# Roots by GpSimd pow, a halved first unit and lighter clock-warming matmuls in a fused spectral filter and gated MLP kernel

## The chip, the cores and the metric

The kernel runs on one core of one Trainium2 chip. The metric is device time in microseconds (us) of one execution. The span of a profile is about 1.7 us shorter than the time of the same execution (before: 177.5 against 179.18). All runs used here are fast runs; the single slow one (a run of the kernel before at 262.98 us, granted clock 0.661) is left out.

## The reference, cut to what matters

```python
xn = layernorm(x)                                   # x: 2048 rows x 512, bf16
A  = irfft2(rfft2(xn) * (w_r + 1j * w_i))           # spectral filter
h  = gelu(xn @ w_gate) * (xn @ w_up)                # 512 -> 1792
out = x + A + h @ w_down                            # 1792 -> 512
```

The kernel does the transforms as matmuls too. The 2048 rows are 16 chunks of 128. Each chunk needs mean and variance (DVE), a reciprocal root `rstd`, the normalised rows `xn`, and their transpose `xnT`. Chunks 0 to 3 are normalised on DVE and transposed on TensorE (PE). Chunks 4 to 15 come in three groups of four: the root and the bias `nb = -mean*rstd` on GpSimd (POOL), `xn` on ACT, the transpose by DMA.

Of the kernel before, what the change touches and what calls it, by code (L numbers as in the profile page):

```python
# [10 lines left out]
P = 128  # L11
# [6 lines left out]
S = 2048  # L18
D = 512
# [182 lines left out]
def kernel(  # L202
# [53 lines left out]
    def load_w(a, b, eng=nc.sync):  # L256
        nc.sync.dma_start(out=Wg_sb[:, :, a:b], in_=wg_v[:, :, a:b])
        eng.dma_start(out=Wu_sb[:, :, a:b], in_=wu_v[:, :, a:b])
# [3 lines left out]
    root = pc.tile([P, 1], F32, name="root")  # L262
    nc.vector.memset(spin[:], 0.0)
    nc.vector.memset(eps_t[:], EPS)
    ident_t = pc.tile([P, P], BF16, name="ident_t")
# [7 lines left out]
    def load_w(T, a, b, eng=nc.sync):  # L273
        v = wg_v if T is Wg_sb else wu_v
        return eng.dma_start(out=T[:, :, a:b], in_=v[:, :, a:b])

    pin = tc.keep_in_program_order
    pin(nc.scalar.activation(out=root[:], in_=eps_t[:], func=AF.Sqrt, bias=eps_t[:], scale=1.0))
    load_x(0, 1)
    load_x(1, 1)  # L280
# [19 lines left out]
    LAND = {0: 2.9, 1: 3.5, 2: 8.8, 3: 8.8}  # L300
    LAND.update({c: 12.6 if c < 8 else 18.5 if c < 12 else 21.5 for c in range(4, NC)})
    WG_LAND = [6.6] * 4 + [10.2] * 4 + [15.0] * 6
    WU_LAND = [8.0] * 4 + [11.7] * 4 + [17.0] * 6
    RF_LAND = 20.0

# [5 lines left out]

    ident = ident_t[:]
# [4 lines left out]
    for k in range(25):  # L317
        pin(nc.tensor.matmul(sp_ps[:, :P if k < 20 else D], lhsT=spin[:], rhs=spin[:] if k < 20 else x_t[:, 0, :],
                             start=True, stop=True))

    def spin_on():
        for k in range(6):
            nc.tensor.matmul(sp_ps[:, :256], lhsT=spin[:], rhs=x_t[:, 0, :256], start=True, stop=True)
# [31 lines left out]
    def rsqrt_steps(U, c0, n):  # L355
        y = rstd[:, c0:c0 + n]
        v = pc.tile([P, n], F32, name=f"v{c0}")
        t = pc.tile([P, n], F32, name=f"t{c0}")

        def first():  # L360
            U.tensor_scalar(out=v[:], in0=mv[:, c0:c0 + n, 1], scalar1=EPS, scalar2=None, op0=ALU.add)
            U.tensor_scalar(out=y.bitcast(I32), in0=v[:].bitcast(I32), scalar1=-0.5, scalar2=float(0x5F1FFFF9),
                            op0=ALU.mult, op1=ALU.add)

        def newton(a, k):
            U.tensor_tensor(out=t[:], in0=y, in1=y, op=ALU.mult)  # L366
            if U is V:
                U.scalar_tensor_tensor(out=t[:], in0=v[:], scalar=-a, in1=t[:], op0=ALU.mult, op1=ALU.mult)
                U.scalar_tensor_tensor(out=y, in0=t[:], scalar=k, in1=y, op0=ALU.add, op1=ALU.mult)
                return  # L370
            U.tensor_tensor(out=t[:], in0=v[:], in1=t[:], op=ALU.mult)
            U.tensor_scalar(out=t[:], in0=t[:], scalar1=-a, scalar2=k, op0=ALU.mult, op1=ALU.add)
            U.tensor_tensor(out=y, in0=t[:], in1=y, op=ALU.mult)

        def bias():
            b = nb[:, c0:c0 + n]
            U.tensor_tensor(out=b, in0=mv[:, c0:c0 + n, 0], in1=y, op=ALU.mult)
            U.tensor_scalar(out=b, in0=b, scalar1=-1.0, scalar2=None, op0=ALU.mult)  # L378

        steps = [first, lambda: newton(0.703952253, 0.703952253 * 2.38924456), lambda: newton(0.5, 1.5)]  # L380
        return steps + ([] if U is V else [bias])
# [3 lines left out]
    def first_two():  # L385
        o = {}

        def v(k, fn, occ, deps=(), lat=None, t_min=0.0):
            o[k] = add("DVE", occ, fn, [o[d] for d in deps], key=-2000 + len(o), lat=lat, t_min=t_min,
                       after=o.get("last"))  # L390
            o["last"] = o[k]

        def root_of(c):
            o["root", c] = add("ACT", 0.31, lambda: A.activation(
                out=rstd[:, c:c + 1], in_=mv[:, c, 1:2], func=AF.Sqrt, bias=eps_t[:], scale=1.0),
                [o["mean", c]], key=-2000 + c)

        def T(c, h):
            o["T", c, h] = add("PE", 0.12, lambda: f_T(c, 2 * h, 2), [o["xn", c, h]], key=-2000 + 2 * c + h,
                               lat=0.36, acq=("S",))  # L400

        def recip(c):
            v(("rstd", c), lambda: V.reciprocal(out=rstd[:, c:c + 1], in_=rstd[:, c:c + 1]), 0.15, [("root", c)])

        def xn_(c, h):
            v(("xn", c, h), lambda: f_norm_v(c, 256 * h, 256), 0.27, [("rstd", c)], lat=0.4)

        def copy(c, h):
            v(("copy", c, h), lambda: f_Tc(c, 2 * h, 2), 0.25, [("T", c, h)], lat=0.4)
            o["copy", c, h].rel = ("S",)  # L410

        def stats(c):
            v(("stats", c), lambda: f_stats(c), 0.6, t_min=LAND[c], lat=0.7)

        def mean(c):
            v(("mean", c), lambda: f_mean(c), 0.1, [("stats", c)])
            root_of(c)

        stats(0)
        mean(0)  # L420
        stats(1)
        recip(0)
        xn_(0, 0)
        mean(1)
        xn_(0, 1)
        table = add("ACT", 1.3, lambda: None, [o["root", 1]], key=-1500, lat=1.3)
        T(0, 0)
        T(0, 1)
        add("PE", 0.65, spin_on, [o["T", 0, 1]], key=-1500, lat=0.65, after=o["T", 0, 1])
        copy(0, 0)  # L430
        copy(0, 1)
        recip(1)
        v("xn1", lambda: f_norm_v(1, 0, D), 0.33, [("rstd", 1)], lat=0.45)
        t = add("PE", 0.23, lambda: f_T(1, 0, NE), [o["xn1"]], key=-1998, lat=0.45, acq=("S",))
        xT_op[0], xn_op[0] = o["copy", 0, 1], o["xn", 0, 1]
        xT_op[1] = add("ACT", 0.5, lambda: f_Tc(1, 0, NE, A.copy), [t, table], key=-1200, rel=("S",))
        xn_op[1] = o["xn1"]

    first_two()
# [5 lines left out]
    hold = {}  # L445

    def second_two():
        m = [moments(c, -1200 + c) for c in (2, 3)]
        steps = rsqrt_steps(V, 2, 2)
        m = [add("DVE", 1.5, lambda: [f() for f in steps], m, key=-1190)]  # L450
        hold[0] = m[0]
        for c in (2, 3):
            xn_op[c] = add("DVE", 0.33, lambda c=c: f_norm_v(c, 0, D), m, key=-1180 + c, lat=0.53)
            hold[1] = xn_op[c]
            t = add("PE", 0.23, lambda c=c: f_T(c, 0, NE), [xn_op[c]], key=-880 + c, lat=0.5, acq=("S",))
            e, f = ("ACT", A.copy) if c == 2 else ("DVE", V.tensor_copy)
            xT_op[c] = add(e, 0.5, lambda c=c, f=f: f_Tc(c, 0, NE, f), [t], key=-1100 + c, rel=("S",))
# [3 lines left out]
    def later_four(c0, km, kx):  # L461
        m = [moments(c, km + 0.1 * c) for c in range(c0, c0 + 4)]
        for k, f in enumerate(rsqrt_steps(nc.gpsimd, c0, 4)):
            m = [add("POOL", (0.8, 1.15, 1.15, 0.7)[k], f, m, key=c0 + k,
                     lat=(0.8, 1.15, 1.15, 0.9)[k])]
        for c in range(c0, c0 + 4):
            xn_op[c] = add("ACT", 0.72, lambda c=c: A.activation(  # L467
                out=xn[:, c, :], in_=x_t[:, c, :], func=AF.Identity, bias=nb[:, c:c + 1],
                scale=rstd[:, c:c + 1]), m, key=kx + 0.1 * c)
            xT_op[c] = add("SP", 1.3, lambda c=c: nc.sync.dma_start_transpose(  # L470
                out=xnT[c // 4][:, :, c % 4, :], in_=xn[:, c, :]), [xn_op[c]], key=c, lat=4.0, t_min=25.0)
# [13 lines left out]
    def unit(k, c0, n, f0, m=1):  # L485
# [21 lines left out]

        def f_ge():
            b["ge"] = pw.tile([P, m, w], BF16, name="ge", bufs=3)
            A.activation(out=b["ge"][:], in_=b["g_ps"][:], func=AF.Gelu_apprx_tanh)  # L510
# [8 lines left out]
        def split(name, tag, W_, key, t, h):  # L519
            o = None  # L520
            for f in range(0, m, h):
# [4 lines left out]
        g = split("g_ps", "G", Wg_sb, 1000 + k, WG_LAND, 2 if k == 0 else m)  # L526
        u = split("u_ps", "U", Wu_sb, 1000.5 + k, WU_LAND, 1 if k == 2 else m)
        ge = add("ACT", {1: 0.28, 2: 0.36, 4: 0.5}[n * m], f_ge, [g], key=-1000 + k,
                 lat={1: 0.38, 2: 0.48, 4: 0.7}[n * m], acq=("ge",), rel=("G",))
        h = add("DVE", {1: 0.21, 2: 0.34, 4: 0.61}[n * m], f_h, [ge, u], key=-1000 + k, rel=("U", "ge"),  # L530
                after=hold.get(k))
# [277 lines left out]
    def down(c):  # L809
# [7 lines left out]
        def mm(o, w):  # L817
            b[o] = ps.tile([P, w], F32, name="y_ps", tag="S", bufs=4)
            for f in range(NFC):
                T_.matmul(b[o][:], lhsT=hT_of(sb, f, 1, cl * P, P)[:, 0], rhs=Wd_sb[:, f, o:o + w],  # L820
                          start=(f == 0), stop=False)
# [11 lines left out]
        for o, w in ((0, D),) if c < NC - 1 else ((0, 256), (256, 128), (384, 128)):  # L833
            k = 2000 + 10 * c + o / D
            m = add("PE", 14 * w * 0.000421, lambda o=o, w=w: mm(o, w), [h_op[c, f] for f in range(NFC)] + [wd],
                    key=k, acq=("S",))
            r = add("PE", w * 0.000421, lambda o=o, w=w: ri_mm(o, w), [m, yt_op[c], ri], key=k + 0.1,
                    lat=w * 0.000421 + 0.3)
            m.lat = m.occ
# [40 lines left out]
```

## The kernel before: the parts that the change and the argument touch

A small planner in the program orders all instructions. It holds estimates of durations (`occ`, `lat`), of when DMAs land (`LAND`, `t_min`) and of buffers, and emits one fixed order for each engine. On the chip each engine then runs its queue in that order: an instruction that comes late holds up all behind it.

The roots, as an integer first guess and two Newton steps:

```python
def first():
    U.tensor_scalar(out=v, in0=mv[:, c0:c0 + n, 1], scalar1=EPS, op0=ALU.add)
    U.tensor_scalar(out=y.bitcast(I32), in0=v.bitcast(I32), scalar1=-0.5, scalar2=float(0x5F1FFFF9), ...)
def newton(a, k):                        # twice; three instructions on DVE, four on GpSimd
    U.tensor_tensor(out=t, in0=y, in1=y, op=ALU.mult)
    U.tensor_tensor(out=t, in0=v, in1=t, op=ALU.mult)
    U.tensor_scalar(out=t, in0=t, scalar1=-a, scalar2=k, op0=ALU.mult, op1=ALU.add)
    U.tensor_tensor(out=y, in0=t, in1=y, op=ALU.mult)
# ... bias(): two instructions
def later_four(c0, km, kx):              # chunks 4 to 15
    m = [moments(c, km + 0.1 * c) for c in range(c0, c0 + 4)]
    for k, f in enumerate(rsqrt_steps(nc.gpsimd, c0, 4)):
        m = [add("POOL", (0.8, 1.15, 1.15, 0.7)[k], f, m, ...)]
    # then xn by ACT (scale=rstd, bias=nb), transposed by DMA
```

A forward step of the spectral part (`forward`, four of them) folds four chunks of `xn` on DVE, does four groups of four matmuls into `bp`, and ACT moves each group out as `Bs`. `bp` shares four PSUM buffers (tag "S") with other tiles, so its fourth group can wait for ACT:

```python
b[q] = bp = ps.tile([P, 4, P], F32, name="bp", tag="S", bufs=4)
for j in range(4):
    T_.matmul(bp[:, j], lhsT=b["xf"][:, j, q, :], rhs=RF_t[:, 4 * cg + j, :], start=True, stop=True)
# ... then A.copy(out=Bs..., in_=bp)
```

A unit of the MLP is a gate product `g_ps`, an up product `u_ps`, a gelu on ACT and their product `hT` on DVE; `u_ps` has two buffers. The start:

```python
load_x(0, 1); load_x(1, 1)
nc.sync.dma_start(out=idx_t[:], ...)     # row indices, 1.5 KB
load_w(Wg_sb, 0, 512); load_w(Wu_sb, 0, 512); load_x(2, 2); ...
for k in range(25):                      # keep PE busy, so that its clock rises
    matmul(sp_ps[:, :P if k < 20 else D], lhsT=spin, rhs=spin if k < 20 else x_t[:, 0, :])
```

## Time and profile before

| what | number | view |
|---|---|---|
| time | 179.22 us median of 3 (178.97 to 179.49) | times |
| PE busy | 172.1 of 177.5 us, 97% | the page, part 1 |
| first gate, first up matmul | 6.34, 7.79 us | timeline of PE |
| start of the last matmul | 174.46 us | timeline of PE |
| real holes of PE between first gate and last matmul | 0.30 us before 7.79, 0.61 us at 40.2 | steps from start to start |

A busy PE hides small holes, because the ends of matmuls are modelled. I counted the steps from one matmul's start to the next. A step of 56, 109 or 216 ns (128, 256 or 512 columns) is a full pipe; the rest of a longer step is a hole. A hole of exactly one more step is a missing record and not a hole (eighteen of 216 ns between the first gate and the last matmul here). At the start of a run a step of 128 columns takes 107 ns until the clock has risen; the texts call that step, and a PE that runs at it, cold, and the 56 ns step warm. The steps agree with what the Trainium skill says of the warm array ("TensorE: Matmul & The Clock Gate", section "Wait — 56ns, not 53.3ns?").

The hole at 40 us, in the timeline of PE (columns: start, busy us, engine, line, operation, out<-in, count; in brackets the idle time before it and what ended it):

```profile
38.73 1.03 PE L505 MATMUL g_ps<-xnT,Wg_sb 128*128 128x512 bf16 x4
39.60 0.83 PE L581 MATMUL bp<-RF_t,xf 128*128 128x128 bf16 x12
40.88 0.38 PE L581 MATMUL bp<-RF_t,xf 128*128 128x128 bf16 x4 [0.45 <-ACT Bs L551]
```

Twelve of sixteen `bp` matmuls run; the last four start 0.67 us after the one before them, where 0.056 would do. They wait for ACT, whose timeline just before is:

```profile
36.41 0.81 ACT L467 ACTIVATE xn<-x_t,nb,rstd 128x512 bf16<-128x512 bf16 x1 [0.92 <-POOL nb L378]
37.13 0.58 ACT L510 ACTIVATE ge<-g_ps 128x512 bf16<-128x512 f32 x1
37.60 0.80 ACT L467 ACTIVATE xn<-x_t,nb,rstd 128x512 bf16<-128x512 bf16 x1
38.31 1.55 ACT L551 CAST Bs<-bp 128x512 bf16<-128x512 f32 x3
39.73 0.62 ACT L510 ACTIVATE ge<-g_ps 128x512 bf16<-128x512 f32 x1
40.22 0.61 ACT L551 CAST Bs<-bp 128x512 bf16<-128x512 f32 x1
```

ACT sat idle for 0.92 us until the bias of the third group came from POOL, and then had a queue of work to get through before the `Bs` that frees the buffer. Some of the twelve POOL instructions of that group:

```profile
31.00 0.58 POOL L361 TENSOR_SCALAR v<-mv 128x4 f32<-128x4 f32 x1 [1.86 <-DVE mv L341]
...
33.98 0.20 POOL L371 TENSOR_TENSOR t<-v,t 128x4 f32<-128x4 f32 x1
34.27 0.71 POOL L372 TENSOR_SCALAR t<-t 128x4 f32<-128x4 f32 x1
35.06 0.72 POOL L373 TENSOR_TENSOR rstd<-t,rstd 128x4 f32<-128x4 f32 x1
35.86 0.20 POOL L377 TENSOR_TENSOR nb<-mv,rstd 128x4 f32<-128x4 f32 x1
36.15 0.23 POOL L378 TENSOR_SCALAR nb<-nb 128x4 f32<-128x4 f32 x1
```

From 31.00 to 36.38 us that is 5.4 us for four numbers per partition.

The start, in the chain that ended last (columns: start, us, what):

```profile
1.71 0.42 SPq L282
2.13 0.04 issue
2.18 0.43 SPq L275
2.61 0.04 issue
2.65 5.09 DMA Wu_sb<-in_B_w_up_dram
7.74 0.05 issue
7.79 1.07 PE u_ps L505 x16
```

The queue issues the row indices (L282), then the first gate weights, then the first up weights, which land at 7.74 us.

### The profile page before, as it was taken

The numbers are of one execution on the slowest core, as the hardware profiler recorded it, in microseconds if no ns is written. First come the engines' busy times: TensorE is split into PE (matmuls) and PEld (weight loads), VectorE is DVE, ScalarE is ACT, GpSimd is POOL, SyncE is SP. The second block draws the span as 40 slices with busy tenths as digits, with TensorE's granted clock in tenths as the row PEclk, the third lists the DMA queues.
The fourth block names the chain that finished last, engine by engine and source line by source line (L and its number), as shares of the span: only waits on it lengthen the run. The fifth ranks groups of instructions, "written<-read, shape, count | busy, mean of one in ns | idle before, by whom it ended". The sixth has DMA issues, their size and how long they took to land.

```text
span 177.5 us, 3118 instructions
## 1 busy us (share of the span) xinstructions
PE 172.1 (97%) x1115; PEld 96.0 (54%) x1133; DVE 116.6 (66%) x261; ACT 96.5 (54%) x171; POOL 20.1 (11%) x60
## 2 busy tenths in 40 slices
PE   7999999998999999999999999999999999999993
PEld 5798845464455554555555545454445444444463
DVE  3499999873933599998699999543526334344333
ACT  4463286979575989799999955453112111211200
POOL 1000534810676000000000000000000000000000
DMA  3999994243282752121202520200132222221212
GB/s 92 350 382 378 368 180 92 59 98 55 60 291 95 245 173 59 33 55 31 63 6 55 148 60 5 59 0 4 51 97 89 72 78 63 89 85 62 78 44 59
DMA packets 21872, 19.36 MB, mean 109 GB/s; under 512 B 8480, under 2 KB 20000, under 8 KB 21856
## 3 DMA queue, kind: packets, MB, share of 16 engines
q1 hardware_dynamic: 21440, 17.84, 34.6%
q0 software_dynamic: 416, 1.32, 2.5%
q8 instruction: 9, 0.15, 0.3%
q14 instruction: 7, 0.06, 0.1%
HBM read 13.38 MB, written 2.10 MB: 87 GB/s over the span
## 4 chain that ended last, share of the span: by engine, by line
PE 83%; ACT 5%; DMA 3%; issue 3%; POOL 2%; DVE 1%; SPq 1%; ACTq 0%
PE y_ps L820 27%; PE u_ps L505 23%; PE g_ps L505 22%; DMA Wu_sb<-in_B_w_up_dram 3%; PE dp L639 2%; ACT Bs L551 2%; PE yp L772 2%; PE gp L742 2%; PE y_ps L824 2%; PE ep L648 2%; ACT xn L467 2%; ACT ge L510 1%; DVE hT L515 1%; PE bp L581 1%; POOL t L366 0%
## 5 line engine op out<-in xcount | busy, mean ns | idle before, releaser
L505 PE MATMUL u_ps<-xnT,Wu_sb 128*128 128x512 bf16 (+2 forms) x267 | 56.9, 341 | 0.3
L505 PE MATMUL g_ps<-xnT,Wg_sb 128*128 128x512 bf16 (+2 forms) x265 | 56.4, 340 | 0.4
L515 DVE TENSOR_TENSOR hT<-u_ps,ge 128x512 bf16<-128x512 f32 x56 | 38.5, 688 | 19.0 <-PE u_ps L505 10.5
L820 PE MATMUL y_ps<-Wd_sb,hT 128*128 128x512 bf16 (+2 forms) x246 | 50.6, 355 | 0.3
L510 ACT ACTIVATE ge<-g_ps 128x512 bf16<-128x512 f32 x56 | 33.9, 606 | 21.4 <-PE g_ps L505 17.6
L505 PEld LDWEIGHTS <-Wu_sb 128*128 128x128 bf16 x272 | 24.9, 98 | 21.4 <-DMA Wu_sb<-in_B_w_up_dram 0.3
L505 PEld LDWEIGHTS <-Wg_sb 128*128 128x128 bf16 x272 | 24.8, 98 | 20.0
L820 PEld LDWEIGHTS <-hT 128*128 128x128 bf16 x252 | 23.2, 98 | 22.4
L778 ACT CAST yf<-yp 128x512 bf16<-128x512 f32 x16 | 9.3, 586 | 40.5 <-PE yp L772 40.5
L827 DVE TENSOR_TENSOR y_sb<-y_ps,y_sb 128x512 bf16<-128x512 f32 (+2 forms) x18 | 11.1, 631 | 30.0 <-PE y_ps L824 30.0
L653 ACT CAST E<-ep 64x512 bf16<-64x512 f32 x32 | 18.6, 580 | 1.3 <-PE ep L648 0.8
L338 DVE BATCH_NORM_STATS2 stats<-x_t 128x6 f32<-128x512 bf16 x16 | 10.5, 677 | 3.9 <-DMA x_t<-in_A_x_dram 3.9
L467 ACT ACTIVATE xn<-x_t,nb,rstd 128x512 bf16<-128x512 bf16 x12 | 9.7, 827 | 1.8 <-POOL nb L378 1.8
L551 ACT CAST Gs<-gp 128x512 bf16<-128x512 f32 x16 | 8.9, 592 | 0.9 <-PE gp L742 0.9
L551 ACT CAST ds<-dp 128x512 bf16<-128x512 f32 x16 | 9.0, 597 | 0.6 <-PE dp L639 0.5
L551 ACT CAST Bs<-bp 128x512 bf16<-128x512 f32 x16 | 8.4, 607 | 0.5 <-PE bp L581 0.5
L784 DVE TENSOR_TENSOR lv<-yf 128x512 bf16<-128x512 bf16 x16 | 6.1, 422 | 1.5 <-ACT yf L778 0.6
L772 PEld LDWEIGHTS <-Gs 128*128 128x128 bf16 x64 | 4.8, 98 | 3.5
L791 DVE TENSOR_TENSOR yt<-lv 128x512 bf16<-128x512 bf16 x16 | 6.1, 422 | 0.3
L824 PE MATMUL y_ps<-yt,RI_t 128*128 128x512 bf16 (+2 forms) x18 | 6.1, 355 | 0.0
L772 PE MATMUL yp<-CT,Gs 128*128 128x128 bf16 x64 | 6.0, 219 | 0.0
L742 PEld LDWEIGHTS <-F 128*128 128x128 bf16 x64 | 4.5, 98 | 2.6
(72 smaller groups left out, 123.2 us busy)
## 6 DMA issues: line engine op xcount, KB each, us to landing
F<-F SPq DMA_DIRECT2D x32, 64.0 KB, 2.0
y_sb<-in_A_x_dram SPq DMA_DIRECT2D x16, 128.0 KB, 2.1
out_dram<-y_sb SPq DMA_DIRECT2D x15, 128.0 KB, 1.7
x_t<-in_A_x_dram SPq DMA_DIRECT2D x7, 256.0 KB, 8.6
Wd_sb<-in_B_w_down_dram SPq DMA_DIRECT2D x1, 1792.0 KB, 7.5
Wg_sb<-in_B_w_gate_dram SPq DMA_DIRECT2D x2, 512.0 KB, 5.2
Wu_sb<-in_B_w_up_dram SPq DMA_DIRECT2D x2, 512.0 KB, 7.4
Wg_sb<-in_B_w_gate_dram SPq DMA_DIRECT2D x1, 768.0 KB, 10.4
```

The source lines that it names most:

```text
L338: V.bn_stats(out=st[:], in_=x_t[:, c, :])
L467: xn_op[c] = add("ACT", 0.72, lambda c=c: A.activation(out=xn[:, c, :], in_=x_t[:, c, :], func=AF.Identity, bias=nb[:, c:c + 1], scale=rst ...
L505: T_.matmul(b[name][:, f], lhsT=W_[:, e, (f0 + f) * P:(f0 + f + 1) * P], rhs=rhs[:, e, :], start=(e == 0), stop=(e == NE - 1))
L510: A.activation(out=b["ge"][:], in_=b["g_ps"][:], func=AF.Gelu_apprx_tanh)
L515: V.tensor_tensor(out=hT_of(sb, f0, m, o, w), in0=b["u_ps"][:], in1=b["ge"][:], op=ALU.mult)
L551: A.copy(out=o, in_=i)
L653: A.copy(out=b["E"][64 * h:64 * h + 64, r], in_=b["ep", h][64 * r:64 * r + 64])
L772: T_.matmul(t[:, q], lhsT=late["G"][:, q, c0 + j], rhs=IQ[q], start=(q == 0), stop=(q == 3), skip_group_check=True)
L778: A.copy(out=b["yf"][:, j], in_=b[j][:])
L820: T_.matmul(b[o][:], lhsT=hT_of(sb, f, 1, cl * P, P)[:, 0], rhs=Wd_sb[:, f, o:o + w], start=(f == 0), stop=False)
L824: T_.matmul(b[o][:], lhsT=late["RI"][:, c, :], rhs=late["yt"][:, c, o:o + w], start=False, stop=True)
L827: V.tensor_tensor(out=b["y"][:, o:o + w], in0=b[o][:], in1=b["y"][:, o:o + w], op=ALU.add)
```

## The change

Its intent: start the first unit as soon as half of its transposed input is there, take the root work off DVE and shorten it on GpSimd, and keep the clock up without waiting for x. No gate, up, down or spectral matmul is added or removed. The core of the diff:

```diff
-    for k in range(25):
-        pin(nc.tensor.matmul(sp_ps[:, :P if k < 20 else D], lhsT=spin[:], rhs=spin[:] if k < 20 else x_t[:, 0, :], ...
+    for k in range(37):
+        pin(nc.tensor.matmul(sp_ps[:, :P], lhsT=spin[:], rhs=spin[:], start=True, stop=True))
 ...
-    def rsqrt_steps(U, c0, n):  ... first, newton, newton, bias
+    def root(c0, n):
+        y = rstd[:, c0:c0 + n]
+        nc.gpsimd.tensor_tensor(out=y, in0=y, in1=minus_half[:, 0:n], op=ALU.pow)
+    def root_eps(c0, n):
+        plus_eps(nc.gpsimd, c0, n)
+        root(c0, n)
 ...
-        steps = rsqrt_steps(V, 2, 2)                                   # chunks 2 and 3, on DVE
-        m = [add("DVE", 1.5, lambda: [f() for f in steps], m, key=-1190)]
+        m = add("POOL", ROOT, lambda: root_eps(2, 2), m, key=-1190, lat=ROOT + 0.1)      # ROOT = 1.1
 ...
-        for k, f in enumerate(rsqrt_steps(nc.gpsimd, c0, 4)):          # chunks 4 to 15
-            m = [add("POOL", (0.8, 1.15, 1.15, 0.7)[k], f, m, key=c0 + k, ...)]
+        m = [add("POOL", ROOT, lambda: root_eps(c0, 4), m, key=c0, lat=ROOT + 0.1)]
+        m = [add("POOL", 0.7, lambda: bias(c0, 4), m, key=c0 + 1, lat=0.9)]
 ...
+        if k == 0:                                                     # first unit
+            g = add("PE", occ / 2, lambda: mm_half(0), [xT_op[0, 0]], key=1000, ...)
+            g = add("PE", occ / 2, lambda: mm_half(1), [xT_op[0], g], key=1000.1, ...)
```

Also: the copy of chunk 1's transpose moves from ACT to DVE, the gates of two neighbouring units go ahead of their ups, the first down product is planned in four pieces, and the planner's landing times are set anew.

More of the change, by code (lines that the diff above doesn't have):

```diff
@@ L261 @@
     spin = pc.tile([P, P], BF16, name="spin")
-    root = pc.tile([P, 1], F32, name="root")
+    warm = pc.tile([P, 1], F32, name="warm")
     nc.vector.memset(spin[:], 0.0)
     nc.vector.memset(eps_t[:], EPS)
+    minus_half = pc.tile([P, 4], F32, name="minus_half")
+    nc.vector.memset(minus_half[:], -0.5)
     ident_t = pc.tile([P, P], BF16, name="ident_t")
@@ L271, in load_x, with load_w @@
         return eng.dma_start(out=x_t[:, c0:c0 + n, :], in_=x_v[:, c0:c0 + n, :])
-    def load_w(T, a, b, eng=nc.sync):
+    def load_w(T, a, b, eng=nc.sync, e=slice(None)):
         v = wg_v if T is Wg_sb else wu_v
-        return eng.dma_start(out=T[:, :, a:b], in_=v[:, :, a:b])
+        return eng.dma_start(out=T[:, e, a:b], in_=v[:, e, a:b])
     pin = tc.keep_in_program_order
-    pin(nc.scalar.activation(out=root[:], in_=eps_t[:], func=AF.Sqrt, bias=eps_t[:], scale=1.0))
-    load_x(0, 1)
-    load_x(1, 1)
+    pin(nc.scalar.activation(out=warm[:], in_=eps_t[:], func=AF.Sqrt, bias=eps_t[:], scale=1.0))
+    pin(load_x(0, 1))
+    pin(load_x(1, 1))
     idx_t = pc.tile([P, 3], I32, name="idx_t")
@@ L299 @@
     load_consts("I0", "M0")
-    LAND = {0: 2.9, 1: 3.5, 2: 8.8, 3: 8.8}
-    LAND.update({c: 12.6 if c < 8 else 18.5 if c < 12 else 21.5 for c in range(4, NC)})
-    WG_LAND = [6.6] * 4 + [10.2] * 4 + [15.0] * 6
-    WU_LAND = [8.0] * 4 + [11.7] * 4 + [17.0] * 6
-    RF_LAND = 20.0
     for T, w_in in ((TR, A_w_r), (TI, A_w_i)):
@@ L310 @@
             nc.sync.dma_start(out=Tf[64 * h:64 * h + 64, W:8 * W], in_=rows[h, :, 0:4, W:8 * W])
+    LAND = {0: 2.9, 1: 3.6, 2: 8.4, 3: 8.4}
+    LAND.update({c: 11.5 if c < 8 else 17.5 if c < 12 else 20.5 for c in range(4, NC)})
+    WG_LAND = [6.3] * 4 + [10.2] * 4 + [13.2] * 6
+    WU_LAND = [7.4] * 4 + [11.7] * 4 + [15.2] * 6
+    RF_LAND = 19.0
     ident = ident_t[:]
@@ L316 @@
     sp_ps = ps.tile([P, D], F32, name="sp_ps", tag="S", bufs=4)
-    for k in range(25):
-        pin(nc.tensor.matmul(sp_ps[:, :P if k < 20 else D], lhsT=spin[:], rhs=spin[:] if k < 20 else x_t[:, 0, :],
-                             start=True, stop=True))
+    for k in range(37):
+        pin(nc.tensor.matmul(sp_ps[:, :P], lhsT=spin[:], rhs=spin[:], start=True, stop=True))
     def spin_on():
         for k in range(6):
-            nc.tensor.matmul(sp_ps[:, :256], lhsT=spin[:], rhs=x_t[:, 0, :256], start=True, stop=True)
+            nc.tensor.matmul(sp_ps[:, :P], lhsT=spin[:], rhs=x_t[:, 0, :P], start=True, stop=True)
     plan = Plan({"S": 4, "G": 2, "U": 2, "ge": 3, "A": 1, "xf": 2, "ds": 4, "E": 2, "X": 2, "Y": 2, "F": 2,
@@ L353, in f_Tc, with plus_eps, bias @@
         copy(out=xnT[0][:, e0:e0 + n, c, :], in_=tiles["T", c, e0][:])
-    def rsqrt_steps(U, c0, n):
+    def plus_eps(U, c0, n):
+        U.tensor_scalar(out=rstd[:, c0:c0 + n], in0=mv[:, c0:c0 + n, 1], scalar1=EPS, scalar2=None, op0=ALU.add)
+    def root(c0, n):
         y = rstd[:, c0:c0 + n]
-        v = pc.tile([P, n], F32, name=f"v{c0}")
-        t = pc.tile([P, n], F32, name=f"t{c0}")
-        def first():
-            U.tensor_scalar(out=v[:], in0=mv[:, c0:c0 + n, 1], scalar1=EPS, scalar2=None, op0=ALU.add)
-            U.tensor_scalar(out=y.bitcast(I32), in0=v[:].bitcast(I32), scalar1=-0.5, scalar2=float(0x5F1FFFF9),
-                            op0=ALU.mult, op1=ALU.add)
-        def newton(a, k):
-            U.tensor_tensor(out=t[:], in0=y, in1=y, op=ALU.mult)
-            if U is V:
-                U.scalar_tensor_tensor(out=t[:], in0=v[:], scalar=-a, in1=t[:], op0=ALU.mult, op1=ALU.mult)
-                U.scalar_tensor_tensor(out=y, in0=t[:], scalar=k, in1=y, op0=ALU.add, op1=ALU.mult)
-                return
-            U.tensor_tensor(out=t[:], in0=v[:], in1=t[:], op=ALU.mult)
-            U.tensor_scalar(out=t[:], in0=t[:], scalar1=-a, scalar2=k, op0=ALU.mult, op1=ALU.add)
-            U.tensor_tensor(out=y, in0=t[:], in1=y, op=ALU.mult)
-        def bias():
-            b = nb[:, c0:c0 + n]
-            U.tensor_tensor(out=b, in0=mv[:, c0:c0 + n, 0], in1=y, op=ALU.mult)
-            U.tensor_scalar(out=b, in0=b, scalar1=-1.0, scalar2=None, op0=ALU.mult)
-        steps = [first, lambda: newton(0.703952253, 0.703952253 * 2.38924456), lambda: newton(0.5, 1.5)]
-        return steps + ([] if U is V else [bias])
+        nc.gpsimd.tensor_tensor(out=y, in0=y, in1=minus_half[:, 0:n], op=ALU.pow)
+    def root_eps(c0, n):
+        plus_eps(nc.gpsimd, c0, n)
+        root(c0, n)
+    def bias(c0, n):
+        U, b = nc.gpsimd, nb[:, c0:c0 + n]
+        U.tensor_tensor(out=b, in0=mv[:, c0:c0 + n, 0], in1=rstd[:, c0:c0 + n], op=ALU.mult)
+        U.tensor_scalar(out=b, in0=b, scalar1=-1.0, scalar2=None, op0=ALU.mult)
     xn_op, xT_op = {}, {}
@@ L391, in v, with T, xn_, stats @@
             o["last"] = o[k]
-        def root_of(c):
+        def T(c, h):
+            o["T", c, h] = add("PE", 0.12, lambda: f_T(c, 2 * h, 2), [o["xn", c, h]], key=-2000 + 2 * c + h,
+                               lat=0.36, acq=("S",))
+        def xn_(c, h):
+            v(("xn", c, h), lambda: f_norm_v(c, 256 * h, 256), 0.27, [("recip", c)], lat=0.4)
+        def stats(c):
+            v(("stats", c), lambda: f_stats(c), 0.6, t_min=LAND[c], lat=0.7)
+        def mean(c):
+            v(("mean", c), lambda: f_mean(c), 0.17, [("stats", c)])
             o["root", c] = add("ACT", 0.31, lambda: A.activation(
@@ L396, in root_of @@
                 [o["mean", c]], key=-2000 + c)
-        def T(c, h):
-            o["T", c, h] = add("PE", 0.12, lambda: f_T(c, 2 * h, 2), [o["xn", c, h]], key=-2000 + 2 * c + h,
-                               lat=0.36, acq=("S",))
         def recip(c):
-            v(("rstd", c), lambda: V.reciprocal(out=rstd[:, c:c + 1], in_=rstd[:, c:c + 1]), 0.15, [("root", c)])
-        def xn_(c, h):
-            v(("xn", c, h), lambda: f_norm_v(c, 256 * h, 256), 0.27, [("rstd", c)], lat=0.4)
-        def copy(c, h):
-            v(("copy", c, h), lambda: f_Tc(c, 2 * h, 2), 0.25, [("T", c, h)], lat=0.4)
-            o["copy", c, h].rel = ("S",)
-        def stats(c):
-            v(("stats", c), lambda: f_stats(c), 0.6, t_min=LAND[c], lat=0.7)
-        def mean(c):
-            v(("mean", c), lambda: f_mean(c), 0.1, [("stats", c)])
-            root_of(c)
+            v(("recip", c), lambda: V.reciprocal(out=rstd[:, c:c + 1], in_=rstd[:, c:c + 1]), 0.15, [("root", c)])
         stats(0)
@@ L425, in first_two @@
         xn_(0, 1)
-        table = add("ACT", 1.3, lambda: None, [o["root", 1]], key=-1500, lat=1.3)
         T(0, 0)
         T(0, 1)
-        add("PE", 0.65, spin_on, [o["T", 0, 1]], key=-1500, lat=0.65, after=o["T", 0, 1])
-        copy(0, 0)
-        copy(0, 1)
-        recip(1)
-        v("xn1", lambda: f_norm_v(1, 0, D), 0.33, [("rstd", 1)], lat=0.45)
+        add("PE", 0.33, spin_on, [o["T", 0, 1]], key=-1500, lat=0.33, after=o["T", 0, 1])
+        table = add("ACT", 1.3, lambda: None, [o["root", 1]], key=-1500, lat=1.3)
+        v("copy0", lambda: f_Tc(0, 0, 2), 0.25, [("T", 0, 0)], lat=0.4)
+        o["copy0"].rel = ("S",)
+        xT_op[0, 0] = o["copy0"]
+        recip(1)
+        v("copy1", lambda: f_Tc(0, 2, 2), 0.25, [("T", 0, 1)], lat=0.4)
+        o["copy1"].rel = ("S",)
+        xT_op[0] = o["copy1"]
+        xn_op[0] = o["xn", 0, 1]
+        v("xn1", lambda: f_norm_v(1, 0, D), 0.33, [("recip", 1)], lat=0.45)
         t = add("PE", 0.23, lambda: f_T(1, 0, NE), [o["xn1"]], key=-1998, lat=0.45, acq=("S",))
-        xT_op[0], xn_op[0] = o["copy", 0, 1], o["xn", 0, 1]
-        xT_op[1] = add("ACT", 0.5, lambda: f_Tc(1, 0, NE, A.copy), [t, table], key=-1200, rel=("S",))
+        o["t"] = t
+        v("copyt", lambda: f_Tc(1, 0, NE), 0.5, ["t"])
+        o["copyt"].rel = ("S",)
+        xT_op[1] = o["copyt"]
         xn_op[1] = o["xn1"]
+    ROOT = 1.1
     first_two()
@@ L443, in moments @@
         return add("DVE", 0.1, lambda: f_mean(c), [s], key=key - 0.5)
-    hold = {}
     def second_two():
         m = [moments(c, -1200 + c) for c in (2, 3)]
-        steps = rsqrt_steps(V, 2, 2)
-        m = [add("DVE", 1.5, lambda: [f() for f in steps], m, key=-1190)]
-        hold[0] = m[0]
+        m = add("POOL", ROOT, lambda: root_eps(2, 2), m, key=-1190, lat=ROOT + 0.1)
         for c in (2, 3):
-            xn_op[c] = add("DVE", 0.33, lambda c=c: f_norm_v(c, 0, D), m, key=-1180 + c, lat=0.53)
-            hold[1] = xn_op[c]
+            xn_op[c] = add("DVE", 0.33, lambda c=c: f_norm_v(c, 0, D), [m], key=-1180 + c, lat=0.53)
             t = add("PE", 0.23, lambda c=c: f_T(c, 0, NE), [xn_op[c]], key=-880 + c, lat=0.5, acq=("S",))
@@ L462, in later_four @@
         m = [moments(c, km + 0.1 * c) for c in range(c0, c0 + 4)]
-        for k, f in enumerate(rsqrt_steps(nc.gpsimd, c0, 4)):
-            m = [add("POOL", (0.8, 1.15, 1.15, 0.7)[k], f, m, key=c0 + k,
-                     lat=(0.8, 1.15, 1.15, 0.9)[k])]
+        m = [add("POOL", ROOT, lambda: root_eps(c0, 4), m, key=c0, lat=ROOT + 0.1)]
+        m = [add("POOL", 0.7, lambda: bias(c0, 4), m, key=c0 + 1, lat=0.9)]
         for c in range(c0, c0 + 4):
@@ L470, in later_four @@
             xT_op[c] = add("SP", 1.3, lambda c=c: nc.sync.dma_start_transpose(
-                out=xnT[c // 4][:, :, c % 4, :], in_=xn[:, c, :]), [xn_op[c]], key=c, lat=4.0, t_min=25.0)
+                out=xnT[c // 4][:, :, c % 4, :], in_=xn[:, c, :]), [xn_op[c]], key=c, lat=4.0, t_min=24.0)
     later_four(4, 10, 5)
@@ L506, in mm, with mm_half @@
                               start=(e == 0), stop=(e == NE - 1))
+        def mm_half(s):
+            if s == 0:
+                b["g_ps"] = ps.tile([P, m, w], F32, name="g_ps", tag="G", bufs=2)
+            for e in (2 * s, 2 * s + 1):
+                for f in range(m):
+                    T_.matmul(b["g_ps"][:, f], lhsT=Wg_sb[:, e, (f0 + f) * P:(f0 + f + 1) * P], rhs=rhs[:, e, :],
+                              start=(e + f == 0), stop=(e == NE - 1), skip_group_check=True)
         def f_ge():
@@ L524, in split @@
             return o
-        g = split("g_ps", "G", Wg_sb, 1000 + k, WG_LAND, 2 if k == 0 else m)
-        u = split("u_ps", "U", Wu_sb, 1000.5 + k, WU_LAND, 1 if k == 2 else m)
+        if k == 0:
+            g = add("PE", occ / 2, lambda: mm_half(0), [xT_op[0, 0]], key=1000, acq=("G",), t_min=WG_LAND[0])
+            g = add("PE", occ / 2, lambda: mm_half(1), [xT_op[0], g], key=1000.1, lat=occ / 2 + 0.3)
+        else:
+            g = split("g_ps", "G", Wg_sb, 1000 + k, WG_LAND, m)
+        u = split("u_ps", "U", Wu_sb, 1003.1 if k == 2 else 1000.5 + k, WU_LAND, (2, m, 1)[k] if k < 3 else m)
         ge = add("ACT", {1: 0.28, 2: 0.36, 4: 0.5}[n * m], f_ge, [g], key=-1000 + k,
                  lat={1: 0.38, 2: 0.48, 4: 0.7}[n * m], acq=("ge",), rel=("G",))
-        h = add("DVE", {1: 0.21, 2: 0.34, 4: 0.61}[n * m], f_h, [ge, u], key=-1000 + k, rel=("U", "ge"),
-                after=hold.get(k))
+        h = add("DVE", {1: 0.21, 2: 0.34, 4: 0.61}[n * m], f_h, [ge, u], key=-1000 + k, rel=("U", "ge"))
         for c in range(c0, c0 + n):
@@ L815, in load, with mm @@
             nc.sync.dma_start(out=b["y"][:], in_=x_v[:, c, :])
-        def mm(o, w):
-            b[o] = ps.tile([P, w], F32, name="y_ps", tag="S", bufs=4)
-            for f in range(NFC):
+        def mm(o, w, fs):
+            if 0 in fs:
+                b[o] = ps.tile([P, w], F32, name="y_ps", tag="S", bufs=4)
+            for f in fs:
                 T_.matmul(b[o][:], lhsT=hT_of(sb, f, 1, cl * P, P)[:, 0], rhs=Wd_sb[:, f, o:o + w],
@@ L834, in down @@
             k = 2000 + 10 * c + o / D
-            m = add("PE", 14 * w * 0.000421, lambda o=o, w=w: mm(o, w), [h_op[c, f] for f in range(NFC)] + [wd],
-                    key=k, acq=("S",))
+            m, n = [h_op[c, f] for f in range(NFC)] + [wd], 1 if c else 4
+            for i in range(n):
+                fs = range(i * NFC // n, (i + 1) * NFC // n)
+                m = [add("PE", len(fs) * w * 0.000421, lambda o=o, w=w, fs=fs: mm(o, w, fs), m, key=k,
+                         acq=() if i else ("S",))]
+                m[0].lat = m[0].occ
+            m = m[0]
             r = add("PE", w * 0.000421, lambda o=o, w=w: ri_mm(o, w), [m, yt_op[c], ri], key=k + 0.1,
                     lat=w * 0.000421 + 0.3)
-            m.lat = m.occ
             t = add("DVE", 0.1 + w * 0.001, lambda o=o, w=w: total(o, w), [r, x], key=k, rel=("S",))
```

## The prediction

> What bounds the kernel now: TensorE. The page gives PE 172.1 us busy of a span of 177.5 (97%); the chain that ended last is 83% PE. In the timeline of PE, steps from one matmul's start to the next are 56 ns for 128 columns and 216 ns for 512, as the Trainium skill states for the warm array ("TensorE: Matmul & The Clock Gate", section "Wait — 56ns, not 53.3ns?"). Between the first gate matmul at 6.34 us and the last matmul at 174.5 us I find two real holes: 0.30 us before 7.79, where the first up matmul waits for the DMA of Wu (landed 7.74), and 0.61 us at 40.2, where a bp matmul waits for the ACT evacuation of Bs. The tail after the last matmul is 3 us. All else is matmul work that the change does not remove.
>
> What the change does:
> 1. First unit halved along its contraction: it needs only half of the transposed chunk 0. But the first gate matmul starts at 6.34 us, its weights landed at 6.27, and the copies of xnT ended at 6.24. An earlier xnT alone gains at most 0.05 us. The next fence is Wu at 7.74: before it PE has half the gate (0.45), four transposes (0.22), the other half (0.45) and then the hole. Unless the second unit's gate is placed ahead of the first up matmuls, the fence stays; from the planner's own times I expect it to stay behind. Gain 0 to 0.3 us.
> 2. 37 narrow spins for 20 narrow and 5 wide: at the cold step of 107 ns (20 took 2.11 us) they end at 5.0 us instead of 5.29. Transposes of chunk 0 start 0.3 us earlier, still before Wg lands, so off the path. PE may idle 0.5 us before 6.3; I expect full clock at the first gate.
> 3. Roots by pow. Chunks 2 and 3: DVE steps from 9.98 to 11.53 us become one add and one pow on POOL. Later groups: ten POOL instructions (19.05 to 22.40, 24.69 to 29.14 us, 0.2 to 0.6 us each) become four. No pow is in this trace; the planner's figure is 1.1 us for add and pow. ACT xn (waits 1.8 us for POOL, in two places) should come 1 to 3 us earlier; DVE is relieved of 1.2 us where it is 5.3 of 5.5 us busy. PE has no hole there, so only the 0.61 us hole can answer; 60% that it shrinks.
> 4. Copy of chunk 1 from ACT to DVE: table load and first gelu come 1 to 2 us earlier; PE waits for neither.
> 5. Gates of a pair first, first down product in four pieces: same matmuls, no hole there.
>
> Sum: minus 0.1 (start), minus 0.4 (hole at 40.2 and its surroundings), plus 0.1 (new small holes of the new order). I predict 178.8 us, range 178.1 to 179.5. Chances: faster by over 2% 0.02, within 2% 0.95, slower by over 2% 0.03.
>
> What would show it: first gate still at 6.3 us; first up still at 7.8; root on POOL about 1 us; hole at 40 us smaller; last matmul 0.1 to 0.9 us earlier; PE busy less by a few tenths (fewer cold spins).
>
> What would make it wrong: a pow of several us, which starves the units of chunks 2 and 3 at 14.4 us (slack about 0.7 us); the clock warming later because the spins are thinner; weights landing at another time; holes from a worse order at 28 to 45 us.

## The result, and the profile after

The kernel after takes 178.43 us median of 4 (178.26 to 178.63), the kernel before 179.27 in the same rounds. The ratio is 0.9955, with a 95% interval of 0.9937 to 0.9973: 0.8 us, or 0.45%, less. (A ratio is the mean time of one kernel's fast runs over that of the other's of the same rounds, so it is not quite the ratio of the medians quoted.)

The lines that answer to those of before. PE at 40 us, ACT before it, and the third group on POOL:

```profile
39.41 1.06 PE L577 MATMUL bp<-RF_t,xf 128*128 128x128 bf16 x16
40.30 1.03 PE L490 MATMUL u_ps<-xnT,Wu_sb 128*128 128x512 bf16 x4
```

```profile
34.82 1.52 ACT L452 ACTIVATE xn<-x_t,nb,rstd 128x512 bf16<-128x512 bf16 x2 [0.68 <-POOL nb L370]
...
38.86 1.08 ACT L547 CAST Bs<-bp 128x512 bf16<-128x512 f32 x2
```

```profile
31.98 0.58 POOL L357 TENSOR_SCALAR rstd<-mv 128x4 f32<-128x4 f32 x1 [5.36 <-DVE mv L342]
32.64 1.45 POOL L361 TENSOR_TENSOR rstd<-rstd,minus_half 128x4 f32<-128x4 f32 x1
34.16 0.29 POOL L369 TENSOR_TENSOR nb<-mv,rstd 128x4 f32<-128x4 f32 x1
34.54 0.24 POOL L370 TENSOR_SCALAR nb<-nb 128x4 f32<-128x4 f32 x1
```

POOL now needs 2.8 us instead of 5.4, although it began a microsecond later. ACT gets the bias 1.6 us earlier (34.82 against 36.41). All sixteen `bp` matmuls run without a break: the hole is gone, and no other hole is left after the first up matmul. The start, in the chain that ended last:

```profile
2.17 0.43 SPq L277
2.61 0.04 issue
2.65 4.91 DMA Wu_sb<-in_B_w_up_dram
7.56 0.04 issue
7.60 1.07 PE u_ps L490 x16
```

The weights were issued at the same time and landed 0.18 us earlier, and the first up matmul moved with them. The account of the two profiles then closes: the last matmul starts at 173.67 instead of 174.46 us, 0.79 us earlier; 0.61 of it is the hole and 0.19 the start. The experiments ask whether both belong to the change.

### The profile page after: what moved, and what is told of

Its sections match the earlier page's. It is cut to its first block, busy times and chain, and to the rows that moved or that the text cites. A ratio compares the mean times of both kernels' runs of the same rounds, so it can differ in the third digit from the quotient of the medians.

```text
span 176.7 us, 3114 instructions
## 1 busy us (share of the span) xinstructions
PE 171.1 (97%) x1127; PEld 96.2 (54%) x1145; DVE 116.1 (66%) x255; ACT 95.9 (54%) x170; POOL 17.2 (10%) x38
## 4 chain that ended last, share of the span: by engine, by line
PE 94%; DMA 3%; SPq 1%; issue 1%; DVE 0%
PE u_ps L490 27%; PE y_ps L817 27%; PE g_ps L490 27%; DMA Wu_sb<-in_B_w_up_dram 3%; PE yp L768 2%; PE gp L738 2%; PE bp L577 2%; PE dp L635 2%; PE y_ps L821 2%; PE ep L644 2%; SPq L273 0%; PE tp L351 0%; SPq L277 0%; SPq L284 0%; DVE y_sb L824 0%
## 5 line engine op out<-in xcount | busy, mean ns | idle before, releaser
L490 PEld LDWEIGHTS <-Wg_sb 128*128 128x128 bf16 x256 | 24.0, 98 | 20.6
L559 DVE TENSOR_TENSOR A<-xn 128x1024 bf16<-128x1024 bf16 x8 | 5.2, 676 | 1.0 <-ACT xn L452 1.0
```

What stands on the lines that cost most here:

```text
L490: T_.matmul(b[name][:, f], lhsT=W_[:, e, (f0 + f) * P:(f0 + f + 1) * P], rhs=rhs[:, e, :], start=(e == 0), stop=(e == NE - 1))
```

## The experiments

Twelve runs, in three jobs of four: ten new kernels, the kernel after once more, and one of the ten again. Each job ran on one chip beside the kernel before (median of its fast runs 179.62, 179.54 and 179.61 us). Names with `b_` start from the kernel before, with `a_` from the kernel after.

**Theory A (arrival)**: the late bias from GpSimd makes ACT late, which makes the hole; pow brings the bias earlier, and that is the gain. **Rival O (order)**: the new planned order makes the gain, and the early bias is not needed. **Rival S (start)**: spins, halved unit and chunk order bring the first up matmul forward.

### Only pow, in the order of before: b_pow_untold

```diff
 # before; later_four only
-            v, guess, newton, newton          # ten GpSimd instructions
+            nc.gpsimd.tensor_scalar(out=y, in0=mv[:, c0:c0 + n, 1], scalar1=EPS, op0=ALU.add)
+            nc.gpsimd.tensor_tensor(out=y, in0=y, in1=minus_half[:, 0:n], op=ALU.pow)
 # costs told to the planner unchanged: PE, ACT and SP orders equal before's; DVE gains one memset
```

> The kernel before, with only the roots of chunks 4 to 15 by pow on GpSimd; the planner is told the old costs, so the order on PE, ACT, DVE and SP is that of before. Theory A (arrival: the late bias from GpSimd makes ACT late, and that makes the 0.61 us hole of PE at 40.2 us): hole under 0.2 us, time 0.4 to 0.65 us below before. Theory O (order: the hole comes from the planned order, not from arrival): hole stays at 0.5 us or more, time within 0.15 us of before. First up matmul: at 7.75 to 7.85 us if the start of before sets the landing of Wu, anywhere from 7.55 to 7.85 if that is chance.

Measured: 179.03 us, ratio 0.9966 (0.9949 to 0.9983). The hole at 40 us is gone:

```profile
31.19 0.58 POOL L389 TENSOR_SCALAR rstd<-mv 128x4 f32<-128x4 f32 x1 [3.40 <-DVE mv L343]
31.86 1.33 POOL L390 TENSOR_TENSOR rstd<-rstd,minus_half 128x4 f32<-128x4 f32 x1
...
33.63 0.23 POOL L380 TENSOR_SCALAR nb<-nb 128x4 f32<-128x4 f32 x1
```

```profile
34.73 0.81 ACT L478 ACTIVATE xn<-x_t,nb,rstd 128x512 bf16<-128x512 bf16 x1
```

```profile
39.95 1.06 PE L592 MATMUL bp<-RF_t,xf 128*128 128x128 bf16 x16
```

The bias is done at 33.86 us instead of 36.38, and ACT starts the third group's `xn` at 34.73 without waiting for it. That is theory A: the same order, an earlier bias, no hole. The traces confirm that the order of PE, ACT and the DMA queue is that of before, instruction by instruction. This profile also has a hole that I had not expected, 0.42 us at 12.05 us:

```profile
11.62 0.71 PE L516 MATMUL g_ps<-xnT,Wg_sb 128*128 128x256 bf16 x5
12.58 0.60 PE L516 MATMUL u_ps<-xnT,Wu_sb 128*128 128x256 bf16 x4 [0.26 <-DVE hT L526]
```

```profile
11.84 0.69 DVE L526 TENSOR_TENSOR hT<-u_ps,ge 128x512 bf16<-128x512 f32 x1
```

The third unit's up product needs a `u_ps` buffer, which DVE frees with the `hT` of the first unit. In the order of before that `hT` stands behind the eight root instructions of chunks 2 and 3, so it moves with the landing of those chunks: here their moments began at 8.83 us and `hT` at 11.84, in the profile of before at 8.44 and 11.46, which was just in time.

### Only the new order, with late data: b_told_only

```diff
 # before, Newton roots kept
-            m = [add("POOL", (0.8, 1.15, 1.15, 0.7)[k], f, m, ...)]
+            m = [add("POOL", (1.1, 0.0, 0.0, 0.7)[k], f, m, ...)]
```

> The kernel before with its Newton roots on GpSimd, but the planner is told that they take 1.1 us: only the order changes, the data come as late as before. Theory A: hole near 40 us of 0.5 us or more (perhaps larger or in two places), time equal to before or up to 0.5 us above. Theory O: hole under 0.2 us, time 0.4 to 0.65 us below before.

Measured: 183.15 us, ratio 1.0205 (1.0184 to 1.0225), 3.5 us slower; I had expected at most 0.5. PE has holes of 0.95, 0.92, 1.39, 0.32 and 0.72 us between 31 and 45 us. Four of them wait for ACT, which stands in a queue whose head waits for POOL (the one of 0.32 us waits for DVE's `xf`). Around the largest:

```profile
39.25 0.81 ACT L467 ACTIVATE xn<-x_t,nb,rstd 128x512 bf16<-128x512 bf16 x1 [2.77 <-POOL nb L378]
39.97 0.57 ACT L510 ACTIVATE ge<-g_ps 128x512 bf16<-128x512 f32 x1
```

```profile
40.60 1.02 PE L505 MATMUL g_ps<-xnT,Wg_sb 128*128 128x512 bf16 x4 [1.23 <-ACT ge L510]
```

The gelu behind the waiting `xn` frees the gate's PSUM buffer, so PE stops. Rival O falls: the order is worth nothing without the early data, and costs much.

### Both: b_pow

The edits of the two above together. The orders of PE, ACT and the DMA queue are those of b_told_only; only the data come earlier.

> The kernel before with pow roots for chunks 4 to 15 and the planner told of it (order of b_told_only, data early). Theories A and O both: no hole over 0.2 us near 40 us, time 0.4 to 0.65 us below before. If it is no better than before, both fall and the gain came from another part.

Measured: 179.01 us, ratio 0.9972 (0.9952 to 0.9993), no hole after the first up matmul. It equals b_pow_untold (179.03): telling the planner adds nothing measurable to pow. With this one edit the kernel before has, from the first up matmul on, the same run as the kernel after: 166.06 us to the last matmul against 166.07. In this profile the clock rose late and the old wide spins lasted until 6.73 us, so the first up matmul started at 7.84 although its weights were there at 7.63; some 0.15 us lost at the start (0.21 less the usual 0.05).

### The change without its later pow: a_newton

```diff
 # after; later_four only
-        m = [add("POOL", ROOT, lambda: root_eps(c0, 4), m, key=c0, lat=ROOT + 0.1)]
+        for k, f in enumerate(newton_steps(nc.gpsimd, c0, 4)):
+            m = [add("POOL", (0.8, 1.15, 1.15)[k], f, m, key=c0, lat=(0.8, 1.15, 1.15)[k])]
```

> The kernel after with Newton roots for chunks 4 to 15 again and the planner told their old costs; everything else of the change stays. Theory A and O: a hole of 0.3 to 0.8 us near 40 us returns, time 0.3 to 0.7 us above after, so 0.1 to 0.5 below before. If no hole returns, the other parts of the change suffice. First up matmul: 7.55 to 7.65 us if the start of the change sets the landing of Wu, anywhere from 7.55 to 7.85 if chance.

Measured: 179.88 us, ratio 1.0033 (0.9999 to 1.0066), not below before as I had expected. The hole comes back, in three parts of 0.12, 0.47 and 0.27 us at 40 us (0.86 together). The other parts of the change do not suffice; without pow they are no gain. (The planner was told the old costs, so this order is not quite that of the kernel after.) The first up matmul was at 7.92 us, its weights landed at 7.87: outside both windows that I had given, and a first sign that the start is chance.

### The kernel after once more: a_again

No edit.

> The kernel after, unchanged: the anchor for the other three on this chip, and a second look at when Wu lands. Time 0.5 to 1.0 us below before; no hole at 40 us; first up matmul between 7.55 and 7.95 us, since the landing of Wu has varied between 7.56 and 8.08 us over six profiles of kernels with the same order of DMAs.

Measured: 179.07 us (178.45 to 180.41), ratio 0.998 (0.9943 to 1.0018). No hole after the first up matmul. But the same program, with the same issue times, had its first weights land much later than in the first profile:

```profile
6.71 1.07 PE L498 MATMUL g_ps<-xnT,Wg_sb 128*128 128x128 bf16 x16 [0.69 <-DMA Wg_sb<-in_B_w_gate_dram]
7.62 0.39 PE L351 MATMUL tp<-ident_t,xn 128*128 128x128 bf16 x4
8.12 1.07 PE L490 MATMUL u_ps<-xnT,Wu_sb 128*128 128x128 bf16 x16
```

First up at 8.12 us instead of 7.60, outside what I had expected. Rival S falls as the cause of the 0.19 us: over the ten profiles with the indices in their old place (before, after and eight experiments), Wu landed at 7.56 to 8.08 us in kernels of either kind, on average at 7.78 us in the four built from before and at 7.80 in the six built from after.

### The old spins in the kernel after: a_old_spins

```diff
-    for k in range(37): ... 128 columns, spin only
+    for k in range(25): ... 20 of 128 columns, 5 of 512 that read x; spin_on with 256 columns
```

> The kernel after with the spins of before (20 narrow, 5 wide that read x, then 6 of 256 columns after the transposes). Theory S (wide spins delay the first gate where the clock warms late): first gate matmul at 6.3 to 6.75 us, later than the landing of its weights by over 0.1 us, and time 0.05 to 0.3 us above a_again. Theory N (spins are off the path): first gate within 0.1 us of the landing of Wg, time within 0.15 us of a_again.

Measured: 178.72 us, ratio 0.9952 (0.9924 to 0.9979); the first gate at 6.20 us, 0.05 behind the landing of Wg at 6.15. In this profile the spins are off the path (theory N). The time is 0.35 us below a_again, where neither theory had it. Of the profiled runs, this one is 0.31 us faster and its first up matmul 0.31 us earlier (7.81 against 8.12), with no hole after it in either; Wu landed that much earlier. The other runs have no profile. In b_pow above the old spins did cost some 0.15 us. So narrow spins may be an insurance, which no timing here can resolve. They do not make sure of a warm clock: in a_newton_dve and a_idx_late, both with narrow spins, the first seven and the first three steps of the gate were still cold.

### Chunks 2 and 3 back on DVE: a_newton_dve

```diff
 # after; second_two only
-        m = add("POOL", ROOT, lambda: root_eps(2, 2), m, key=-1190, lat=ROOT + 0.1)
+        steps = newton_steps(V, 2, 2)
+        m = add("DVE", 1.5, lambda: [f() for f in steps], m, key=-1190)
```

> The kernel after with the roots of chunks 2 and 3 by Newton on DVE again, those of chunks 4 to 15 stay pow. Theory D (DVE at 10 to 12 us matters: gated product of the first unit is late, so a buffer of u_ps comes free late): a hole of 0.2 to 0.8 us in PE between 11.5 and 14.5 us, time 0.2 to 0.8 us above a_again. Theory L (only the later roots matter): no hole over 0.1 us there, time within 0.2 us of a_again.

Measured: 180.23 us, ratio 1.0032 (1.0007 to 1.0057), 1.2 us above a_again by the medians, more than either theory had. There are two groups of holes, 0.90 us at 14.4 us and 0.74 us at 39 to 40 us:

```profile
13.98 0.61 PE L351 MATMUL tp<-ident_t,xn 128*128 128x128 bf16 x8
15.33 0.94 PE L513 MATMUL g_ps<-xnT,Wg_sb 128*128 128x256 bf16 x7 [0.74 <-DVE xnT L354]
```

The first is not the one that theory D named: the planner now puts the transposes of chunks 2 and 3 behind the up products of units 2 and 3, and the next unit waits for their copies. The second I had not expected at all. The planner also moved the spectral groups: the third `bp` group now stands behind 132 gate and up matmuls (counted in 512 columns), in after behind 140. PE reaches it at 38.79 us instead of 39.41, while the bias from POOL is no earlier (35.02 against 34.78). This run mixes an order and a cost; it shows that pow for the later groups does not prevent the hole when the order asks for the data earlier still.

### The indices later: a_idx_late

```diff
 # after
-    nc.sync.dma_start(out=idx_t[:], ...)      # between x and Wg
     load_w(Wg_sb, 0, 512); load_w(Wu_sb, 0, 512); ...
+    nc.sync.dma_start(out=idx_t[:], ...)      # behind all of x and the weights
```

> The kernel after with the small load of the row indices (issued between x and Wg, needed only near 42 us) moved behind the loads of x and the weights; order of all other engines is the same. Theory I (the first weights are bound by the time of issue): Wg and Wu are issued 0.47 us earlier and land 0.3 to 0.5 us earlier, first gate at 5.9 us (then bound by the copies of xnT), first up at 7.1 to 7.4 us, time 0.25 to 0.5 us below a_again. Theory R (bound by the rate of the DMA engines): landings within 0.15 us of a_again and no gain.

Measured: 178.11 us (178.04 to 178.72), ratio 0.992 (0.9894 to 0.9946). Wg and Wu were issued at 1.71 and 2.18 us, landed at 5.82 and 7.30; first up at 7.39, where PE had just ended its work before it and had no hole. The first gate was at 6.09 and not at 5.9, because the six spins behind the transposes still ran at the cold step and held PE. The mean of its runs over that of a_again's is 0.9943 (178.21 over 179.24), 1.0 us; I had expected at most 0.5, and part of this is a_again's luck: its profiled run had the latest Wu but one (8.07 us).

### Halving undone: a_whole and a_idx_whole

```diff
-        if k == 0:          # g in two halves along the contraction
+        if False:           # g in one piece, like every other unit
```

> The kernel after with the gate of the first unit in one piece, behind both copies of xnT. Theory W (the first gate is bound by the landing of its weights, at 6.1 to 6.7 us so far, while both copies end by 5.9): first gate within 0.1 us of the landing of Wg, time within 0.3 us of after on the same footing (0.2 to 0.9 us below before). Theory H (halving is worth its while): first gate 0.2 us or more behind the landing, time 0.2 us or more above the kernel after.

> As a_whole, with the row indices loaded late. Now Wg lands near 5.8 us, before the second copy of xnT ends (near 6.0). Theory H: first gate 0.1 to 0.3 us later than in a_idx_late_2, time up to 0.25 us above it. Theory W: the transposes, spins and clock set the start anyway, time within 0.15 us of a_idx_late_2.

Measured: a_whole 179.00 us, ratio 0.9969 (0.9952 to 0.9986); a_idx_whole 178.69 us, ratio 0.9953 (0.9933 to 0.9974). In a_whole the first gate is at 6.47 us, 0.05 behind its weights (6.42): halving gives nothing at the start, as theory W has it. In a_idx_whole the gate is at 6.20 us with weights there at 5.78; the copies of `xnT` ended at 6.04 and 6.36 us in that profile. What held the first gate matmul there was the last spin (its step ended at 6.20); a later one then waited 0.10 us for the second copy. The first up matmul is nevertheless bound by Wu (landed 7.68, started 7.72). Both profiles have a hole of 0.22 us at 40 us. The planner gives these kernels a slightly different order of ACT, DVE and, later on, PE, so what halving is worth here seems to be an accident of order; no run takes that apart further. a_idx_whole is 0.33 us above a_idx_late_2, more than either theory had; its hole is 0.22 us.

### The indices later in the kernel before: b_idx_late; and the anchor a_idx_late_2

The same move of one line, in the kernel before, and a_idx_late again.

> The kernel before with nothing but the row indices loaded late; order of all other engines the same. First up at 7.4 to 7.7 us instead of 7.8. If the chain of moments, GpSimd roots and ACT does not move with the start, the hole at 40 us grows by the gain at the start (to 0.8 to 1.0 us) and the time stays within 0.2 us of before; if it moves along, the hole stays at 0.5 to 0.7 us and the time falls by 0.2 to 0.5 us.

> a_idx_late once more, as the anchor for the three others on this chip: no hole at 40 us, first up at 7.3 to 7.5 us, time 1.1 to 1.6 us below before.

Measured: b_idx_late 179.25 us, ratio 0.9979 (0.9963 to 0.9995): 0.36 us below before by the medians, and the hole stays at 0.59 us. Whether the chain behind it moves along with the start the profile cannot tell, because in it the start hardly moved: Wu landed at 7.71 and the first up matmul was at 7.76 instead of 7.79, outside what I had expected. It has the hole at 12 us again (0.24 us; `hT` of the first unit at 11.69). a_idx_late_2 178.36 us, ratio 0.993 (0.9915 to 0.9945), 1.25 us below before as expected; but in its profile Wg landed at 6.59 and Wu at 8.01, in spite of the early issue, and the first up matmul was at 8.05 and not at 7.3 to 7.5. So the move helps on average in these runs, and does not bind the landing; by which path it helps is not shown.

### The account of all profiles

With no hole after the first up matmul, the time of the profiled execution less the start of the first up matmul is 170.75 to 170.80 us in six profiles. Every other profile exceeds 170.78 by its holes:

| kernel | time, profiled run | first up | difference | above 170.78 | holes after first up |
|---|---|---|---|---|---|
| before | 179.18 | 7.79 | 171.39 | 0.61 | 0.61 at 40 |
| after | 178.40 | 7.60 | 170.80 | 0.02 | none |
| a_again | 178.88 | 8.12 | 170.76 | -0.02 | none |
| b_pow | 178.60 | 7.84 | 170.76 | -0.02 | none |
| b_pow_untold | 178.91 | 7.74 | 171.17 | 0.39 | 0.42 at 12 |
| b_told_only | 183.20 | 8.13 | 175.07 | 4.29 | 4.30, 31 to 45 |
| a_newton | 179.57 | 7.92 | 171.65 | 0.87 | 0.86 at 40 |
| a_newton_dve | 180.24 | 7.80 | 172.44 | 1.66 | 0.90 at 14, 0.74 at 39 |
| a_whole | 178.90 | 7.93 | 170.97 | 0.19 | 0.22 at 40 |
| b_idx_late | 179.36 | 7.76 | 171.60 | 0.82 | 0.24 at 12, 0.59 at 40 |
| a_idx_late | 178.14 | 7.39 | 170.75 | -0.03 | none |
| a_idx_late_2 | 178.85 | 8.05 | 170.80 | 0.02 | none |

(a_old_spins: 178.57, 7.81, 170.76, none. a_idx_whole: 178.70, 7.72, 170.98, 0.22 at 40.) So two things alone set the time of these fourteen profiled runs: when the first up matmul starts, and how long PE stands after it.

A version that was faster than both kernels in these jobs is a_idx_late: 178.11 and 178.36 us in two jobs, ratios to before 0.992 and 0.993, where the kernel after had 0.9955 and 0.998. Five of its six runs in the job that it shared with a_again are below all of a_again's.

## Why the prediction was right

The time (178.8 predicted, 178.43 measured) lies in the range, and the size of the gain was right in kind: small, because PE was full. The sum was too small by half, minus 0.4 against a measured minus 0.8: the hole gave 0.21 more than foretold, the new holes did not come (0.1), and the start gave 0.09 more. The 0.19 of the start is luck, so the change itself is worth the 0.61 of the hole. The terms:

- **Hole at 40 us, minus 0.4**: the mechanism was right and the term too small. I gave the hole a 60% chance to shrink; it vanished, 0.61 us, and b_pow_untold shows that pow alone does it. This is the term of the sum that was mis-sized.
- **New holes, plus 0.1**: none came in the kernel after. The risk was real, as b_told_only, a_newton_dve and a_whole show with 4.30, 1.64 and 0.22 us of holes.
- **Start, minus 0.1**: "Unless the second unit's gate is placed ahead of the first up matmuls, the fence stays": right. It was not placed so, and the first up matmul waits for Wu in either kernel. The 0.19 us of the first two profiles came from the landing of Wu, which varies by 0.5 us in the same program; that is luck and not the change's doing. For the same reason the first gate and first up matmul were at 6.13 and 7.60, and not "still" at 6.3 and 7.8.
- **"An earlier xnT alone gains at most 0.05 us"**: right; a_whole starts its first gate 0.05 us behind the landing of Wg.
- **Root on POOL about 1 us**: add and pow took 0.25 and 0.73 us for two columns, 0.24 and 1.04 us for four, 0.58 and 1.45 us where DVE was busy with two-input work. ACT's `xn` came 1.6 to 2.5 us earlier (22.96 to 21.15, 29.17 to 26.66, 36.41 to 34.82), within the 1 to 3 foretold.
- **"PE has no hole there"** (about the DVE roots at 10 to 12 us): true of the profile of before, and too narrow a reading. PE was at the edge: two of the five profiles with the DVE order of before have a hole of 0.42 and 0.24 us at 12 us. In the kernel after `hT` of the first two units runs at 9.97 us, ahead of everything that waits for chunks 2 and 3, and no profile of it has that hole. How often the executions of before pay it, the times alone do not tell.
- **"Ten POOL instructions" become four**: there were twelve; I had miscounted, and the chain's length, which I had read from the trace, was right.
- **Table load and first gelu 1 to 2 us earlier, PE waits for neither**: the first gelu moved from 9.14 to 7.24 us, the table load by 2.5 us (7.85 to 5.33), and no hole of PE answered to them.
- **PE busy less by a few tenths**: it was 1.0 us less (172.1 to 171.1), without weight: spins are busy time and not work.

What stays open: why the landing of the first gate weights varies so much, 6.09 to 6.67 us when issued at 2.18 and 5.78 to 6.59 us when issued at 1.71. The Trainium skill gives HBM latency as 0.2 us on average and up to 2 us at high load ("DMA: Bandwidth & Descriptors", section "Latency and other measured facts"); no run here shows that this is the cause.

## What to carry to other kernels

When the main engine is 97% busy, list its real holes from start-to-start steps and follow each back, past the engine that released it, to the one that was late: here PE waited for ACT, ACT was late because of twelve tiny GpSimd instructions, and replacing ten of them by two was worth the whole hole. In a kernel with fixed queues, the order and the arrival of data are one thing: an order planned for data 2 us earlier than they come costs more (3.5 us) than the early data gain (0.6 us). And treat a DMA landing that ends the start-up as a variable, not a constant, before crediting a change with it; a small load that nobody needs soon is better placed behind the first weights than ahead of them (it was faster so in both kernels here).

## What the Trainium skill lacked or had wrong

- "GPSIMD Engine Reference", sections 3 and 4 (and no other page that I found): no duration for `pow` by `tensor_tensor` on GpSimd. Measured here: 0.73 us for 128x2 and 1.04 us for 128x4 fp32 when undisturbed, against 0.20 us for a multiply of 128x4. At four columns one pow beats the nine instructions of guess and Newton steps (19.37 to 21.80 us in the first group of before, 2.4 us).
- "GPSIMD Engine Reference", section "1. Specifications", says that the SBUF interfaces are shared with VectorE and contended by DVE instructions with two SBUF inputs. The trace agrees, and shows the size, which the page lacks: the 0.20 us step became 0.71 and 0.72 us at 34.27 and 35.06 us, and ended at 34.97 and 35.78 us; the DVE instructions with two bf16 SBUF inputs that covered them ran 34.24 to 34.92 and 35.03 to 35.72 us. A tiny GpSimd instruction that begins while one runs ends just after it, while one that had begun before it kept its 0.2 us (32.51 us, with the DVE instruction from 32.61 on). So a chain of twelve can lose 2 us (5.4 us against 3.35 us for the first group).
- "TensorE: Matmul & The Clock Gate", section "What's actually happening", says that the clock rises in a free-running window, so its moment varies. The traces agree that the moment varies; that the window is free-running no run here shows. The section gives 0.5 us either way, and here it was more: in two profiles of the same program the step of 128 columns fell from 107 to 56 ns at 6.5 us (a_idx_late) and at 4.0 us (a_idx_late_2). The section puts the cost as under 1% of a typical kernel's span. What it lacks is the cost in the start-up: six spins of 256 columns took 0.65 us of PE in the profile of before (warm) and 1.0 us in that of b_pow (mostly cold), for the same instructions from 5.7 us on, and the first gate matmul came at 6.73 instead of 6.34 us.
- No page that I found tells how much the landing of the first large loads of a kernel varies: 7.56 to 8.08 us for the same 512 KB issued at 2.65 us.
